# Attention followed by a gelu feed-forward on one core: weight sums loaded at another place, output tiles joined by a column order, stores at another place, nineteen added products

## The chip, the cores and the metric

The kernel runs on one core of one Trainium2 chip. The metric is the device time of one execution in microseconds (us). Before the change it was 924.78 us, the median of 3 runs (924.69 to 926.21).

The engines are called by short names. PE is TensorE (matrix products, and PEld its weight loads), DVE is VectorE, ACT is ScalarE, POOL is GpSimd, SP is SyncE. SP and ACT can issue DMA transfers, each from its own queue, in the order in which they stand there. PE writes its products to PSUM banks; the other tiles lie in SBUF.

## The reference

What is computed is an attention in which a query sees only the keys of its own cluster, and then a feed-forward layer on its output:

```python
# q, k, v: (4, 8, 768, 64); centroids: (8, 16, 64)
q_assign = argmax(einsum(q / |q|, c / |c|)); k_assign = argmax(einsum(k / |k|, c / |c|))
scores = where(q_assign[..., :, None] == k_assign[..., None, :], q @ k.T / 8, -1e9)
x = softmax(scores) @ v            # reshaped to (4 * 768, 8 * 64) = (3072, 512)
h = x @ w_in                       # w_in: (512, 2048)
g = h * sigmoid(1.702 * h)
out = g @ w_out                    # w_out: (2048, 512), out: (3072, 512)
```

All inputs and the output are float32. The weights arrive as 8-byte numbers and are brought to float32 by the kernel.

## The kernel before

The program has two stages. They are written out by hand in the order in which each engine's instructions are to stand (`manual_schedule`); a tile framework adds the waits. There is no planner. Line numbers are those of the kernel before.

**Attention**, up to about 349 us. It runs over 16 pairs of heads (`NPAIR`), each pair with its two halves of 384 queries and 6 tiles of 128 keys. One step `t` handles two key tiles: `scores` (L453) makes the score products, `part` (L467 for the first pair, L476 for the others) adds a large term that removes other clusters, `exps` (L484, ACT) takes the exponential, `add_up` (L502, POOL) sums it over the keys, `values` (L518) multiplies by v. For the first pair the preparation stands ahead of the loop: transposes of q and k (L315), products with the centroids (L341), a copy by ACT (L347), transposes back (L355), and then, after the scores of the first two tiles, `prep_hot` (L419), which transposes the one-hot tile `hot` and has `hots` copied by DVE and ACT (L424, L426). In between, the generator `rounding` (L180) turns one piece of a weight after the other to float32: pieces 0 to 15 are `w_in`, pieces 16 to 31 are rows of `w_out` with all their 512 columns. Its last step is the add at L203.

**Feed-forward**, one batch b of 768 rows after the other, 4 in all. Both products are made by a scheme with 7 products in place of 8 (two halves of each of three dimensions), which needs sums of input tiles and of weight tiles.

- `first7(b, f)` (L815), for 8 values of f: the seven products of the first layer, 14 matmuls at L822. DVE adds the PSUM results into G (L813), ACT applies the gelu (L827). Sums of the input x stand in the tiles Tx2, Tx3 and Tx4 (`T_of`) and, as T1, in x itself; they are made by `sums_x` (L608) in the order T3, T1, T2, T4. POOL makes the sums of w_in (`sums_w`).
- `second49(k)` (L858), for 7 values of k: each is again a scheme of seven products, 28 in all at L872, written as `product(bank, n, start)` with n from 1 to 7. It uses six PSUM banks in turn. The order of the outer products is `ORDER = (1, 7, 3, 2, 6, 5, 4)`. ACT copies the first result of a bank into a tile y and PE then goes on adding to that bank. For k = 0 the tile y is Y22 itself. The results go to the four output tiles Y11, Y12, Y21, Y22, by additions on POOL. Sums of G for the next k are made by `sums_t` into temporary tiles (among them E0, E1, E2 and Tx2 to Tx4), sums in G itself by `sums_G`, both on DVE at three places within `second49`, called `extra(0)`, `extra(1)` and `extra(2)`.
- **The inner weight sums.** For each k three sums of blocks of w_out are needed. In batch 0, beside `first7` with f from 3 to 7, `keep_w(k)` (L747) makes them on POOL, in the tiles Y12, Y21 and Y22, and SP stores each to memory (`kept_w`, L757). `load_sums(k)` (L761) loads them back into the tile `Wz`, of which there are two. Before the change the first two loads stand behind the last `keep_w`, after the loop over f.
- **The output.** `store(b, n, m, q)` (L918) transposes one half m of an output tile on DVE (L929), 32 by 32 elements at a time, and issues four DMAs on SP (L933), one for each group of 32 partitions. In the order of w_out's columns, each piece that is contiguous in memory is 32 numbers long. Y11 is stored beside k = 5. In batches 0 to 2 the other three tiles are stored beside the next batch's `first7` (`pend`). In the last batch Y12 and Y22 are stored at k = 6, and Y21 in parts, the last after the last product.

The sums of x for the next batch (`x_steps`) are made on DVE at k = 5 and k = 6.

## Time and profile before

| What | Value |
|---|---|
| Median of 3 runs | 924.78 us (924.69 to 926.21) |
| The profiled execution's own time | 924.83 us |
| Its span, first to last instruction | 923.0 us |
| Mean granted clock of PE | 0.984 |
| PE busy | 885.7 us, 96% of the span |
| DVE busy | 714.5 us, 77% |
| POOL busy | 485.0 us, 53% |
| ACT busy | 363.4 us, 39% |
| DMA | 204031 packets, 80.57 MB |
| Packets under 512 bytes | 180136 |

The profile is taken in one execution; its span is shorter than that execution's time by 1.83 us, which lie before the first and after the last instruction. A slice is one fortieth of the span. A digit gives the busy share of an engine in that slice, in tenths; in the row PEclk it gives the clock that was granted to PE. In a row of waits the figures are the sum, the number and the longest. In a row of the timeline the figures are the start, the length, the engine (SPq and ACTq are the queues from which SP and ACT issue), the line, the operation, the tile written and the tile read, and at the end how long the engine was idle before it and what ended that.

### The profile page before, as it was taken

Reading aid. Unit: us, or ns where it says so; the run is one execution under the profiler, and the core shown is the slowest. Engines: PE = TensorE matmul, PEld = TensorE weight load, DVE = VectorE, ACT = ScalarE, POOL = GpSimd, SP = SyncE. Lnnn points to the kernel's source line nnn. Section 1 sums busy time; section 2 is a strip of 40 time slices with the busy share of each in tenths; the row PEclk is TensorE's granted clock in tenths of the full one; section 3 lists DMA queues with packets and bytes.
Section 4 is the critical chain, followed back from the end, with each engine's and each line's share of the span. In section 5 each row is a group of like instructions: output and inputs, shape, how many; then the busy total and the mean of one; then the engine's idle time right before and its main releaser. Section 6 shows DMA issues by size and latency. Waiting matters only on the chain.

```text
span 923.0 us, 17802 instructions
## 1 busy us (share of the span) xinstructions
PE 885.7 (96%) x6693; PEld 578.3 (63%) x6693; DVE 714.5 (77%) x1165; ACT 363.4 (39%) x816; POOL 485.0 (53%) x469
## 2 busy tenths in 40 slices
PE   6999999999999999996999999999999999999991
PEld 2344444444444445555997557997557996558991
DVE  3999999998999997997797557797556796557791
ACT  3677767776667673231112222111322112222110
POOL 5799989989999898695132211132221133210140
PEclk8999999999999999998999999999999999999996
DMA  9375556666653210036323112223113123111224
GB/s 183 96 134 109 101 117 137 147 126 137 137 130 100 83 42 18 23 115 236 106 69 94 18 22 84 93 69 95 18 26 103 69 72 92 25 18 35 80 69 62
DMA packets 204031, 80.57 MB, mean 87 GB/s; under 512 B 180136, under 2 KB 186400, under 8 KB 203936
## 3 DMA queue, kind: packets, MB, share of 16 engines
q1 hardware_dynamic: 203792, 79.31, 36.5%
q8 instruction: 55, 0.90, 0.4%
q14 instruction: 40, 0.33, 0.1%
q10 hardware_dynamic: 144, 0.03, 0.0%
HBM read 62.61 MB, written 16.70 MB: 86 GB/s over the span
## 4 chain that ended last, share of the span: by engine, by line
PE 77%; DVE 6%; POOL 4%; DMA 3%; issue 3%; SPq 2%; ACT 2%; ACTq 0%; DVEq 0%; POOLq 0%
PE b L822 27%; PE b L872 24%; PE s L453 11%; PE o L518 8%; POOL Y L579 3%; PE m L535 2%; PE s L476 2%; ACT A L484 1%; DMA raw<-in_moe_w_out_dram 1%; DVE G L579 1%; SPq L404 1%; PE m L329 1%; DMA raw<-in_moe_w_in_dram 1%; POOL W L579 1%; DMA line<-row 1%
## 5 line engine op out<-in xcount | busy, mean ns | idle before, releaser
L502 POOL TENSOR_TENSOR sum<-sum,A 128x384 f32<-128x384 f32 x252 | 263.9, 1082 | 38.0 <-ACT A L484 23.8
L813 DVE TENSOR_TENSOR G<-b,G 128x384 f32<-128x384 f32 x224 | 123.0, 556 | 98.1 <-PE b L822 88.5
L484 ACT ACTIVATE A<-s 128x768 f32<-128x768 f32 x192 | 144.7, 804 | 96.6 <-PE s L476 77.8
L579 POOL TENSOR_TENSOR Y<-y,Y 128x768 f32<-128x768 f32 x28 | 63.2, 2267 | 207.5 <-DVE y L813 183.5
L453 PE MATMUL s<-T,T 64*64 64x384 f32 x1536 | 145.8, 495 | 2.7 <-ACT A L484 0.7
L827 ACT ACTIVATE G<-G 128x384 f32<-128x384 f32 x128 | 66.3, 523 | 198.4 <-DVE G L813 197.0
L518 PE MATMUL o<-A,inv 64*64 64x384 f32 x1536 | 142.1, 486 | 0.0
L579 POOL TENSOR_TENSOR W<-w_in 128x256 f32<-128x256 f32 x32 | 23.6, 736 | 161.7 <-PE b L822 161.4
L453 PEld LDWEIGHTS s<-T,T 64*64 64x64 f32 x1536 | 52.4, 132 | 80.0 <-ACT A L484 52.5
L579 DVE TENSOR_TENSOR G<-G 128x768 f32<-128x768 f32 (+1 forms) x88 | 95.8, 1111 | 0.0
L822 PE MATMUL b<-x,W 128*128 128x384 f32 x256 | 93.0, 486 | 0.0
L822 PE MATMUL b<-Tx,w_in 128*128 128x384 f32 x256 | 93.0, 486 | 0.0
L822 PE MATMUL b<-x,w_in 128*128 128x384 f32 x256 | 88.5, 486 | 0.0
L518 PEld LDWEIGHTS o<-A,inv 64*64 64x64 f32 x1536 | 58.6, 134 | 39.2 <-issue 34.4
L822 PEld LDWEIGHTS b<-x,W 128*128 128x128 f32 x256 | 48.6, 190 | 33.9
L822 PEld LDWEIGHTS b<-Tx,w_in 128*128 128x128 f32 x256 | 48.6, 190 | 33.9
L822 PEld LDWEIGHTS b<-x,w_in 128*128 128x128 f32 x256 | 48.5, 190 | 33.5 <-issue 0.6
L872 PE MATMUL b<-E,Wz 128*128 128x192 f32 x256 | 47.5, 336 | 7.3 <-DMA Wz<-kept_w 7.3
L872 PE MATMUL b<-G,w_out 128*128 128x192 f32 x288 | 50.3, 326 | 0.0
L872 PEld LDWEIGHTS b<-E,Wz 128*128 128x128 f32 x256 | 43.8, 197 | 8.5 <-ACT Y L882 7.6
L872 PEld LDWEIGHTS b<-G,w_out 128*128 128x128 f32 x288 | 47.4, 190 | 1.5 <-ACT G L827 0.3
L822 PE MATMUL b<-Tx,W 128*128 128x384 f32 x128 | 46.5, 486 | 0.0
(163 smaller groups left out, 1365.1 us busy)
## 6 DMA issues: line engine op xcount, KB each, us to landing
Wz<-kept_w SPq DMA_DIRECT2D x84, 256.0 KB
raw<-in_moe_w_in_dram SPq DMA_DIRECT2D x16, 512.0 KB
raw<-in_moe_w_out_dram SPq DMA_DIRECT2D x16, 512.0 KB
inv<-in_v_dram SPq DMA_DIRECT2D x16, 384.0 KB
in<-in_q_dram SPq DMA_DIRECT2D x60, 96.0 KB
in<-in_k_dram SPq DMA_DIRECT2D x60, 96.0 KB
kept_w<-Y SPq DMA_DIRECT2D x21, 256.0 KB
kept<-x SPq DMA_DIRECT2D x24, 192.0 KB
```

The source lines that it names most:

```text
L329: nc.tensor.matmul(out=ps[r:r + SQ, w * NJ * SQ:(w + 1) * NJ * SQ] .rearrange("p (j t) -> p j t", t=SQ), lhsT=cT[:, p % HP].rearrange("p a ...
L453: nc.tensor.matmul(out=ps[c:c + D, a, 0:HALF], lhsT=T[p, 1][rows, kt * P + c:kt * P + c + D], rhs=T[p, 0][rows, h * HALF:(h + 1) * HALF], ...
L476: nc.tensor.matmul(out=s_of[u][c:c + D, a, :], lhsT=rows_of[1, p % 2][rows, kt * P + c:kt * P + c + D], rhs=rows_of[0, p % 2][rows, h * HA ...
L484: nc.scalar.activation(out=A_of[u], in_=s_of.pop(u), func=AF.Exp, scale=SCALE)
L502: nc.gpsimd.tensor_tensor(out=sum_of[g][:, a], in0=(A_of[u - 1] if kt == 1 else sum_of[g])[:, a], in1=A_of[u][:, a], op=ALU.add)
L518: nc.tensor.matmul(out=o_of[g][a * D:(a + 1) * D, r, 0:HALF], lhsT=v_in[p][rows, a, kt, :], rhs=A[rows, a, :], start=(kt == 0), stop=(kt = ...
L535: nc.tensor.matmul(out=ps[a * D:(a + 1) * D, 0:HALF], lhsT=twos, rhs=sm[:, a, :], start=(i == 0), stop=(i == len(parts) - 1))
L579: engine.tensor_tensor(out=o, in0=a, in1=b, op=(ALU.add if op == "+" else ALU.subtract))
L813: nc.vector.tensor_tensor(out=o, in0=p, in1=a, op=ALU.add)
L822: nc.tensor.matmul(out=ps[:, 0:HALF], lhsT=a[:, c], rhs=x(c), start=(c == 0), stop=(c == 1))
L827: nc.scalar.activation(out=g, in_=g, func=AF.Gelu_apprx_sigmoid, scale=2.0)
L872: nc.tensor.matmul(out=ps, lhsT=A[n][:, f], rhs=M[n][:, f], start=start and f == 0, stop=(f == FQ - 1), skip_group_check=True)
```

## The change

It has six parts.

1. `rounding` writes the pieces of w_out with their columns in another order: column r * 128 + n * 32 + t goes to place n * 128 + r * 32 + t. The tiles of the output so hold the columns of a half m beside those of the other half: for each group r of 32 partitions, the two halves together are 64 contiguous columns.
2. `store` transposes both halves of a tile into one tile with the halves side by side, and issues four DMAs for both, with pieces of 64 numbers, where there were eight. It can share its DMAs out to two queues. The transposed tile is Tx3 for Y11, and E0, E1 and E2 for Y12, Y22 and Y21 of batches 0 to 2; in the last batch Tx3, Tx4 and Tx2.
3. Y11 is stored at the end of k = 4. The sums of x are spread over k = 5 and k = 6 in groups of 2, 2 and 4.
4. In the last batch, Y12 and Y22 are stored at the first two places of k = 6, Y21 in three parts on the queues of SP and ACT, and the additions into the output tiles of k = 4 and k = 5 are made on DVE, not on POOL.
5. `load_sums(0)` and `load_sums(1)` are issued within the loop over f, at f = 5 and f = 6.
6. `keep_busy(n)` makes n products of a bf16 identity with itself, 512 columns each, whose result nobody reads: 6 ahead of the first transpose, 3 after the centroid products, 6 ahead of `prep_hot` and 4 after it.

```diff
--- before.py
+++ after.py
@@ -200,6 +200,10 @@
         nc.vector.scalar_tensor_tensor(out=e, in0=lo, scalar=2.0 ** -52, in1=e,
                                        op0=ALU.mult, op1=ALU.mult)
         yield
+        if i >= NW // 2:
+            w, a, e = (w.rearrange("p (n r t) -> p r n t", r=P // SQ, t=SQ),
+                       *(x.rearrange("p (r n t) -> p r n t", r=P // SQ, t=SQ)
+                         for x in (a, e)))
         nc.vector.tensor_tensor(out=w, in0=a, in1=e, op=ALU.add)
 
         check_w(i, raw, w_chunks[NW - 1][0] if i < NW - 1 else raw.bitcast(
@@ -280,6 +284,16 @@
                                 op0=ALU.mult)
     cT = const.tile([P, HP, 2, NC], FP32, name="cT")
     nc.vector.memset(cT, 0.0)
+    idle = ps_o.tile([P, 2, 512], FP32, name="o")
+
+    def keep_busy(n):
+        for _ in range(n):
+            nc.tensor.matmul(
+                out=idle[:, 0, :], lhsT=ident_h,
+                rhs=ident_h[:, None, :].broadcast_to((P, 4, P)),
+                start=True, stop=True)
+
+    keep_busy(6)
     cps = bank()
     nc.tensor.transpose(out=cps[:, 0:P], in_=cc.rearrange("p a d -> p (a d)"),
                         identity=ident)
@@ -645,12 +659,16 @@
         prep(p, i)
         if p == 0 and i in (1, 3):
             load_w(i // 2)
+        if (p, i) == (0, 4):
+            keep_busy(3)
     for t in range(NT + 2):
         us = range(2 * t, 2 * t + 2) if t < NT else ()
         for u in us:
             scores(u)
         if t == 0:
+            keep_busy(6)
             prep(0, 6)
+            keep_busy(4)
         for u in us:
             part(u)
         for u in us:
@@ -855,7 +873,7 @@
             for _ in sums_t(0, slice(f - FQ, f - FQ + 1)):
                 pass
 
-    def second49(k, extra):
+    def second49(k, extra, last):
 
         i = ORDER[k]
         a, g, t, w = W_of(i), G_of(i), temps(k), W.pop(k)
@@ -906,33 +924,33 @@
             return
         nc.scalar.copy(y21, x)
         extra(2)
-        pool = nc.gpsimd
+        pool = nc.vector if last and i in (6, 5) else nc.gpsimd
         sums(pool, {1: (), 7: ((Y[21], y, "+", Y[22]),),
                     3: ((Y[12], y, "+", Y[22]),),
                     2: ((Y[11], y, "+", Y[22]),),
                     6: ((Y[12], y, "+", Y[12]), (Y[21], y, "+", Y[21])),
                     5: ((Y[12], y, "+", Y[12]), (Y[22], y, "+", Y[21]))}[i])
 
-    spare = [0]
-
-    def store(b, n, m, q=slice(0, 2)):
+    def store(b, n, m=slice(0, 2), q=slice(0, 2), queues=(nc.sync,)):
 
         h, t = divmod(n, 10)
         h, t = h - 1, t - 1
-        cols = slice(q.start * QT, q.stop * QT)
-        if b < B - 1:
-            o = ep.tile([P, HALF], FP32, name="o", bufs=1)
-        else:
-            o = T_of[2 + spare[0] // 2][:, spare[0] % 2]
-            spare[0] = (spare[0] + 1) % 6
-        o = o[:, cols]
-        nc.vector.transpose(out=o, in_=Y[n][:, m, cols])
-        rows = out[b * S + t * HALF + cols.start:b * S + t * HALF + cols.stop]
-        for r in range(0, P, SQ):
-            at = (2 * h + m) * P + r
-            nc.sync.dma_start(
-                out=rows[:, at:at + SQ].rearrange("(j t) i -> t j i", t=SQ),
-                in_=o[r:r + SQ].rearrange("t (j i) -> t j i", i=SQ))
+        o = {11: T_of[3], 12: E[0], 22: E[1], 21: E[2]} if b < B - 1 else {
+            11: T_of[3], 12: T_of[3], 22: T_of[4], 21: T_of[2]}
+        o = o[n].rearrange("p a t -> p (a t)").rearrange(
+            "p (j m i) -> p j m i", m=2, i=SQ)
+        at, to = q.start * QT, q.stop * QT
+        o = o[:, at // SQ:to // SQ]
+        for one in range(m.start, m.stop):
+            nc.vector.transpose(out=o[:, :, one], in_=Y[n][:, one, at:to])
+        rows = out[b * S + t * HALF + at:b * S + t * HALF + to]
+        for r in range(P // SQ):
+            col = r * P + (2 * h + m.start) * SQ
+            queues[r % len(queues)].dma_start(
+                out=rows[:, col:col + (m.stop - m.start) * SQ].rearrange(
+                    "(j t) i -> t j i", t=SQ),
+                in_=o[r * SQ:(r + 1) * SQ, :, m].rearrange(
+                    "t j m i -> t j (m i)"))
 
     okt = const.tile([1, 1], FP32, name="okt")
     bad = const.tile([1, 1], I32, name="bad")
@@ -976,10 +994,9 @@
                 for k in {3: (0,), 4: (1, 2), 5: (3,), 6: (4, 5),
                           7: (6,)}[f]:
                     keep_w(k)
+                if 5 <= f < 7:
+                    load_sums(f - 5)
         after7(FB - 1)
-        if b == 0:
-            load_sums(0)
-            load_sums(1)
         if b < B - 1:
             for h in range(2):
                 for hp in range(HP):
@@ -990,28 +1007,25 @@
         else:
             made = iter(())
 
-        def stores(b, *todo):
+        def stores(b, *todo, **how):
             for n in todo:
-                for m in range(2):
-                    store(b, n, m)
-                    yield
+                store(b, n, **how)
+                yield
+
+        both = dict(queues=(nc.sync, nc.scalar))
 
         def tail():
-            store(b, 21, 0)
-            store(b, 21, 1, slice(1, 2))
+            for n in (12, 22):
+                store(b, n)
+                yield
+            store(b, 21, slice(0, 1), slice(0, 1), **both)
+            store(b, 21, q=slice(1, 2), **both)
             yield
 
         def chain(*todo):
             for steps in todo:
                 yield from steps
 
-        def mixed(one, two):
-            for _ in one:
-                yield
-                for _ in range(3):
-                    next(two, None)
-                    yield
-
         def sums_of_x():
             for XT[:] in made:
                 yield
@@ -1021,10 +1035,9 @@
 
         for k in range(7):
             nxt = sums_t(k + 1) if k < 6 else iter(())
-            more = {1: sums_G(6), 3: sums_G(5), 4: sums_G(4),
-                    5: mixed(stores(b, 11), x_steps),
-                    6: chain(x_steps, stores(b, 12, 22), tail()) if final else
-                    x_steps}.get(k, iter(()))
+            more = {1: sums_G(6), 3: sums_G(5),
+                    4: chain(sums_G(4), stores(b, 11)), 5: x_steps,
+                    6: tail() if final else x_steps}.get(k, iter(()))
             if b == B - 1 and k < 2:
                 test(k)
             if (b, k) == (B - 1, 6):
@@ -1032,17 +1045,17 @@
 
             def extra(at):
                 do(nxt, (2, 1, 1)[at])
-                do(more, ((3, 1, 1) if final else (3, 3, 3))[at] if k == 6
-                   else (0, 3, 3)[at] if k == 5 else (0, 2, 2)[at])
-
-            second49(k, extra)
+                do(more, ((1, 1, 1) if final else (0, 4, 4))[at] if k == 6
+                   else (0, 2, 2 + (k == 4))[at])
+
+            second49(k, extra, final)
             if k < 5:
                 load_sums(k + 2)
             elif b < B - 1:
                 load_sums(k - 5)
         pend = () if final else stores(b, 12, 22, 21)
         if final:
-            store(b, 21, 1, slice(0, 1))
+            store(b, 21, slice(1, 2), slice(0, 1), **both)
     return is_bad
 @with_exitstack
 def general(
```

## The prediction

> **What bounds the kernel now.** I read the page's slices first, then the waits of TensorE (PE), then stretches of the timeline where those waits stand.
>
> ```profile
> PE   6999999999999999996999999999999999999991
> PEclk8999999999999999998999999999999999999996
> ...
> PE b L872 <- DMA Wz<-kept_w: 7.3, 1, 7.3
> PE m L284 <- DVE cT L282: 4.9, 1, 4.9
> PE m L419 <- DVE hot L375: 1.4, 1, 1.4
> ```
>
> PE is busy in 37 of 40 slices (each 23 us). Only the first slice, the one at 415 to 438 us and the last have holes. All of PE's listed waits sum to under 17 us; the rest of the hole is after its last matmul (about 903.5 of a 923.0 us span). So a faster DVE, ACT or DMA in the middle gives nothing: what counts is PE's start, one stall, and what follows PE's end. The change touches all three, and edits the order of DVE's work in between.
>
> **Start: the clock.** I cut the beginning where the granted clock changes (columns: PE, PEld, DVE, ACT, POOL busy, then PEclk, DMA share, GB/s):
>
> ```profile
> 8.66:12.07 3.41, 2.84 (x27) 0.96 (x21) 1.11 (x2) 0.68 (x2) 3.20 (x5) 1.00 1.48 178
> 12.07:15.48 3.41, 1.15 (x18) 0.74 (x16) 3.32 (x6) 0.80 (x1) 1.17 (x2) 1.00 1.21 235
> 15.48:18.90 3.42, 2.84 (x20) 0.88 (x20) 1.31 (x2) 1.51 (x2) 0.00 (x0) 0.50 1.18 220
> 18.90:22.31 3.41, 3.41 (x24) 0.93 (x20) 0.00 (x0) 1.51 (x2) 1.21 (x2) 0.50 1.37 176
> ```
>
> After a stretch with PE busy 1.15 of 3.41 us (it waited 1.36 us for `hot`, 0.90 us for `hots`) the clock is half for 6.8 us, and the same 16 score matmuls that took 1.52 us at 10.80 take 2.84 us at 16.83. The 19 added products (6, 3, 6 and 4) stand in these holes. They have no row. Nearest by kind are the 12 products of L419, 128 columns in bf16: 0.86 us, 0.072 us each with start-up; nearest by length are the one-pass costs behind L822, where 384 float32 columns take 0.32 us, hence at most 0.43 us for 512 and, if bf16 needs half the passes, 0.21 us. I take 0.21 us, since four times the L419 cost less its start-up is near it; 0.43 us is the upper bound. The first six (1.3 us, at most 2.6) start when `ident_h` is there at 1.57 and end before the first transpose at 4.92: covered. Three (0.64 us) stand in the 0.57 us wait for the copy at L347: 0.1 us late. Six (1.28 us) fill the 1.36 us wait, four (0.85 us) the 0.90 us wait. Cost: about 0.15 us on the path; at 0.43 us each it would be 0.7 + 1.2 + 0.8 = 2.7 us.
>
> What a full clock gives: following the queue from 15.44, the part products take 0.50 instead of 0.82 us, the exponentials follow 0.3 us sooner, scores of the next two tiles end at 18.25, their part at 18.75, the 16 value products (1.52 instead of 2.46) at 20.25, so the score group at 23.53 starts near 21.0: 2.5 us, less 0.15, **2.4 us**. It passes on: in each later 20.5 us period PE is busy over 20.3 us, while DVE and POOL hold 18.5, so nothing else takes over. The Trainium skill ("TensorE: Matmul & The Clock Gate", What's actually happening, and its closing table) says that the half clock follows an idle window of about 3.4 us and that only gaps over some 3 us matter. By that rule these products buy nothing, because the gaps are 1.36 and 0.90 us, and the sum would be 2.4 us smaller. The rows speak against its threshold: a window one third full was enough. I follow the rows.
>
> **The inner weight sums.** The 21 stores of `keep_w` and the loads after them share SP's queue. Moving `load_sums(0)` and `load_sums(1)`, three loads each, ahead of the last `keep_w` calls delays those stores by 6 issues of some 0.4 us, but they wait for POOL anyway.
>
> ```profile
> 426.83 1.38 POOL L579 TENSOR_TENSOR Y<-w_out,Y 128x512 f32<-128x512 f32 x1
> 428.60 2.81 SPq L764 DMA_DIRECT2D Wz<-kept_w  x6
> 429.19 0.36 DVE L579 TENSOR_TENSOR E<-Y,G 128x192 f32<-128x192 f32 x1
> 430.37 0.32 ACT L882 COPY Y<-b 128x192 f32<-128x192 f32 x1 [6.70 <-DMA kept_w<-Y]
> 431.65 4.64 PE L872 MATMUL b<-E,Wz 128*128 128x192 f32 x16 [7.34 <-DMA Wz<-kept_w]
> ```
>
> The load goes, but the 7.3 us do not. For the first product the output tile `y` is Y22 itself, which is also the staging tile of the last `keep_w` sum. POOL finishes that at 428.21, its store lands at 430.3, and only then may ACT copy PSUM to Y22 (its row names that DMA). PE's next product adds to the same PSUM bank, so it waits for this copy: 430.37 + 0.32 = 430.69. PE can start at about 430.75 instead of 431.65. Gain **0.9 us**. The half clock after the stall stays (16 products in 4.64 us against 2.76 elsewhere): 6.4 us of idle are still long.
>
> **Transitions to the next batch.** Output of Y11 moves from product k=5 to the end of k=4, into Tx3, and the x sums then write Tx3 first.
>
> ```profile
> 478.78 5.05 DVE L579 TENSOR_TENSOR G<-G 128x768 f32<-128x768 f32 x2
> 488.93 4.46 POOL L579 TENSOR_TENSOR Y<-y,Y 128x768 f32<-128x768 f32 x2 [5.92 <-DVE y L813]
> 489.54 2.18 DVE L579 TENSOR_TENSOR x<-x 128x384 f32<-128x384 f32 x1
> 494.00 1.01 DVE L579 TENSOR_TENSOR Tx<-x 128x384 f32<-128x384 f32 x2
> 495.92 1.45 PE L822 MATMUL b<-Tx,W 128*128 128x384 f32 x4
> ```
>
> DVE has no hole here, and Tx2 is ready at 495.01, 0.9 us before PE needs it. In the new order: two transposes (0.57 us, overlapped 0.5) end at 484.9; four issues at 0.47 + 0.05 us end at 487.0; landing takes 1.4 (a 3 KB store) to 1.9 us (below), so 488.4 to 488.9. DVE, after four sums and two small adds, arrives at 488.3 and waits 0.1 to 0.6 us. Queued behind it: two Tx3 sums, the add into y that starts POOL, the sum E2, the x sums. POOL starts near 490.0 instead of 488.93; a two-input DVE sum beside it ends only as POOL's operation does (2.18 and 1.67 us for 0.5 of work), so the x sums end near 494.9 and, after two adds, Tx2 near 496.3. PE wants its halves at 495.92 and 496.28: 0 to 0.4 us late, **0.2 us** taken, three times: +0.6. The sums that PE's last products need (E0, E1, E2) stay 0.9 us or more ahead. Bounds: 0, and 1.3 us if DVE waits 0.9 us longer.
>
> The pairs of transposes in the next batch's first groups (1.1 us at once) find 0.73 us of DVE idle in every 1.29 us and six PSUM banks; without that cover each could hold PE up to 0.5 us. The permuted write of the rounded w_out has no row; the plain one takes 0.69 us. Even at double cost, two in a period add 1.4 us to DVE's 18.5 of 20.5 us: no cost taken.
>
> **The tail.**
>
> ```profile
> 896.33 22.10 SPq L933 DMA_DIRECT2D out_dram<-Tx  x36
> 902.04 1.46 PE L872 MATMUL b<-E,w_out 128*128 128x192 f32 x8
> 904.13 0.32 DVE L813 TENSOR_TENSOR Y<-b,Y 128x192 f32<-128x192 f32 x1
> 905.77 0.38 DVE L929 STREAM_TRANSPOSE Tx<-Y 128x192 f32<-128x192 f32 x1 [1.32 <-DMA out_dram<-Tx]
> ```
>
> SP issues 36 stores at 0.61 us each, to 918.43; 4.57 us later the span ends. DVE finished at 906.2: the issue is the bound (the DMA share is 0.3 to 0.65). The new order has 4 stores for Y11 at k=4, 4 each for Y12 and Y22, and 12 for Y21 over SP and ACT. DVE in k=4 of this batch loses POOL's competition (5.06 us of G sums become 1.82) and gains four Y sums of 0.94: even. Y12 is transposed by 899.7 and issued by 901.9; y's last quarter but one comes from PE at 900.9, so Y22 is transposed by 902.7 and Y21's parts at 904.0, 904.7 and, after PE's end, 905.4. SP unhindered would end at 907.0. But in the built order SP's third and fourth Y22 stores wait for ACT's first two stores to land (one semaphore lane serves both, one DMA after the other): ACT issues at 904.05 to 904.8 (0.35 each for a half), landing 1.87 later as in the trace (a store issued by 903.77 frees its tile at 905.64), so SP goes on at 906.3: two at 0.52, six at 0.4, end 909.7. Gain 918.43 - 909.7 = **8.7 us**; bounds 11.4 (no such wait) and 7.5 (landing 2.5 us).
>
> **Sum.** -2.4 - 0.9 + 0.6 - 8.7 = -11.4 us. Profiled execution 924.83 (span 923.0 and 1.83 around it), 0.05 above the median of 924.78. **Predicted 913.4 us.**
>
> **Rivals.** (1) *DVE's new wait on the Tx3 stores becomes PE's*: for it, DVE's gapless row; against, landing in 1.4 to 1.9 us. At 1.3 us a transition: 913.4 + 3.3 = 916.7. (2) *The added products don't hold the clock* or cost what they win; the skill's threshold speaks for it, the one-third window against: 915.8. (3) *The 7.3 us stall goes wholly*, with its half clock (6.4 + 1.8 more): 905.2; the ACT row speaks against it. (4) *Slower*: the same wait of DVE on Tx3, if 48 KB in pieces of 256 bytes land 6.1 us after the last issue: each us beyond 1.9 costs three, 4.2 us a transition, 926.0; it decides from 5.7 us on. Against it: 1.87 us measured in a full queue.
>
> **Numbers.** Forecast 0.63, rival 1 0.18, rival 2 0.11, rival 3 0.04, rival 4 0.03, 0.01 for no difference. 910.0 to 917.0 holds the first three with the tail's bounds. Faster 0.96, same 0.01, slower 0.03; 0.2% (1.8 us) is about what runs of this kernel can tell (924.69 to 926.21).
>
> **What would show it.** Clock 1.00 until 424 us and the first full score period 2 to 2.5 us sooner; the stall still over 6 us, released by ACT's copy to Y22; DVE idle at the Tx3 sum for under 0.6 us, named after the store; last store issued some 6 us after PE's end. Wrong: a half clock before 30 us, PE waiting for Tx2, or SP issuing 12 us after PE's end.

## The result, and the profile after

The changed kernel took 915.19 us (median of 5 runs, 913.93 to 918.32) where the kernel before took 925.18 us in the same comparison (5 runs, 924.69 to 926.21). The ratio is 0.9893, with a 95% interval of 0.9871 to 0.9914. The forecast was 913.4 us with a range of 910 to 917. One of the five runs lies outside that range. The later experiments point to the reason: the kernel has a wait that the prediction did not see, and it comes and goes between executions.

The profiled execution took 914.16 us, with a span of 912.4 us. Lines of the changed kernel are those of the kernel before plus 14 to 18 (L872 is now L890, L882 is L900, L453 is L467, L579 is L593, L822 is L840, L933 is L949, L764 is L782).

The page's slices, after:

```profile
PE   8999999999999999997999999999999999999994
PEclk9999999999999999998999999999999999999998
```

PE's waits (sum, number, longest):

```profile
PE b L890 <- ACT Y L900: 6.4, 1, 6.4
PE o L291 <- DVE ident_h L245: 1.6, 1, 1.6
```

The clock digit of the first slice rose from 8 to 9. The one long wait is still there at 6.4 us, but it is now named after ACT's copy. The last slice is less empty.

The four stretches in which the clock had been lost (columns as before: PE, PEld, DVE, ACT, POOL busy, granted clock, DMA share, GB/s):

```profile
8.66:12.07 3.41, 3.41 (x30) 1.22 (x27) 0.90 (x2) 0.91 (x2) 3.14 (x6) 1.00 1.38 174
12.07:15.48 3.41, 3.41 (x30) 1.51 (x22) 3.31 (x7) 0.67 (x1) 1.39 (x2) 1.00 1.18 237
15.48:18.90 3.42, 2.68 (x30) 0.69 (x28) 1.54 (x2) 1.74 (x4) 0.00 (x0) 1.00 1.16 227
18.90:22.31 3.41, 3.41 (x50) 1.39 (x48) 1.05 (x2) 1.41 (x2) 2.56 (x3) 1.00 1.37 175
```

The timeline of PE over the added products and the first full score group:

```profile
1.63 2.74 PE L291 MATMUL o<-ident_h 128*128 128x512 bf16 x6 [1.63 <-DVE ident_h L245]
...
9.92 0.82 PE L291 MATMUL o<-ident_h 128*128 128x512 bf16 x3
...
12.48 1.47 PE L291 MATMUL o<-ident_h 128*128 128x512 bf16 x6
...
14.70 1.04 PE L291 MATMUL o<-ident_h 128*128 128x512 bf16 x4
...
16.91 1.58 PE L467 MATMUL s<-T,T 64*64 64x384 f32 x16 [0.74 <-ACT A L498]
...
21.09 1.52 PE L467 MATMUL s<-T,T 64*64 64x384 f32 x16
```

The six products ahead of `prep_hot` take 1.47 us, 0.245 us each, close to the 0.21 us taken in the prediction. The first six take 0.46 us each, more than its upper bound of 0.43 us, but they end at 4.37, before PE's next work at 5.14, and cost nothing. The clock is 1.00 in all four stretches, and the score group that began at 23.53 begins at 21.09, 2.44 us sooner. From the score group before it (16.83 and 16.91) the way there shrank from 6.70 to 4.18 us.

A clock of 1.00 in such a row can also mean that the trace has no record. The changed kernel's clock records begin only at 9.20 us, and PE works at half its later pace before: 0.46 us for a product that takes 0.245 us afterwards.

The add that now writes w_out in another order takes 0.69 us (L207), as it did before, so that part cost nothing.

The timeline of the stall at the start of the second products, and of one transition to the next batch:

```profile
428.01 0.32 ACT L900 COPY Y<-b 128x192 f32<-128x192 f32 x1 [6.66 <-DMA kept_w<-Y]
428.39 4.85 PE L890 MATMUL b<-E,Wz 128*128 128x192 f32 x16 [6.38 <-ACT Y L900]
...
475.11 6.59 POOL L593 TENSOR_TENSOR Y<-y,Y 128x768 f32<-128x768 f32 x2 [7.12 <-DVE y L831]
475.72 1.82 DVE L593 TENSOR_TENSOR G<-G 128x768 f32<-128x768 f32 x2
478.52 1.92 SPq L949 DMA_DIRECT2D out_dram<-Tx  x4
480.55 11.19 SPq L782 DMA_DIRECT2D Wz<-kept_w  x9
485.07 2.76 PE L890 MATMUL b<-E,Wz 128*128 128x192 f32 x16
```

PE restarts at 428.39 instead of 431.65; 2.44 us of that come from the start, 0.82 us from the earlier load. The wait is now for the copy to Y22, and the copy for the store of the last kept sum. In the transition DVE's two sums in G take 1.82 us and POOL's additions 6.59 us. Before the change it was 5.05 us on DVE; POOL's addition beside these sums took 4.85 us. This turns out to matter.

The end, first the timeline, then the wait of SP's queue for earlier stores after 895 us:

```profile
896.29 11.27 SPq L949 DMA_DIRECT2D out_dram<-Tx  x14
900.97 3.61 ACTq L949 DMA_DIRECT2D out_dram<-Tx  x6
```

```profile
SPq L949 <- DMA out_dram<-Tx: 2.0, 2, 1.8
```

PE ends at 900.45 (before: 903.50), SP's last store is issued at 907.56 (before: 918.43) and the span ends at 912.36 (before: 923.03). From PE's end to the span's end it was 19.53 us and is 11.91 us. So of the profile's 10.67 us, 2.44 come from the clock, 0.82 from the load and 7.62 from the end, and 0.21 are lost again by the half clock after the stall (16 products in 4.85 us instead of 4.64).

### The profile page after: what moved, and what is told of

Same layout as the page of the kernel before. It is cut to its first block, busy times and chain, and to the rows that moved or that the text cites. A ratio compares the mean times of both kernels' runs of the same rounds, so it can differ in the third digit from the quotient of the medians.

```text
span 912.4 us, 17739 instructions
## 1 busy us (share of the span) xinstructions
PE 888.9 (97%) x6712; PEld 580.8 (64%) x6712; DVE 712.0 (78%) x1170; ACT 363.2 (40%) x816; POOL 481.1 (53%) x465
## 4 chain that ended last, share of the span: by engine, by line
PE 82%; DVE 5%; POOL 4%; DMA 3%; issue 2%; SPq 2%; ACT 2%; ACTq 0%; DVEq 0%; POOLq 0%
PE b L840 28%; PE b L890 28%; PE s L467 11%; PE o L532 9%; POOL Y L593 3%; PE m L549 2%; PE s L490 2%; ACT A L498 1%; DMA raw<-in_moe_w_out_dram 1%; SPq L418 1%; PE m L343 1%; DMA raw<-in_moe_w_in_dram 1%; POOL W L593 1%; DMA line<-row 1%; DVE x L570 1%
## 5 line engine op out<-in xcount | busy, mean ns | idle before, releaser
L593 POOL TENSOR_TENSOR Y<-y,Y 128x768 f32<-128x768 f32 x24 | 59.4, 2483 | 186.8 <-DVE y L831 162.9
L467 PE MATMUL s<-T,T 64*64 64x384 f32 x1536 | 144.6, 491 | 2.6 <-ACT A L498 0.9
L593 POOL TENSOR_TENSOR W<-w_in 128x256 f32<-128x256 f32 x32 | 23.5, 735 | 164.5 <-PE b L840 164.2
L467 PEld LDWEIGHTS s<-T,T 64*64 64x64 f32 x1536 | 52.3, 132 | 78.6 <-ACT A L498 51.5
L840 PE MATMUL b<-x,W 128*128 128x384 f32 x256 | 93.0, 486 | 0.0
L840 PE MATMUL b<-Tx,w_in 128*128 128x384 f32 x256 | 93.0, 486 | 0.0
L840 PE MATMUL b<-x,w_in 128*128 128x384 f32 x256 | 88.5, 486 | 0.0
L593 DVE TENSOR_TENSOR G<-G 128x768 f32<-128x768 f32 (+1 forms) x88 | 84.3, 980 | 0.0
L840 PEld LDWEIGHTS b<-x,W 128*128 128x128 f32 x256 | 48.6, 190 | 33.9
L840 PEld LDWEIGHTS b<-Tx,w_in 128*128 128x128 f32 x256 | 48.6, 190 | 33.9
L840 PEld LDWEIGHTS b<-x,w_in 128*128 128x128 f32 x256 | 48.5, 190 | 33.5 <-issue 0.6
L890 PE MATMUL b<-E,Wz 128*128 128x192 f32 x256 | 47.7, 337 | 6.4 <-ACT Y L900 6.4
L890 PE MATMUL b<-G,w_out 128*128 128x192 f32 x288 | 50.3, 326 | 0.1
L890 PEld LDWEIGHTS b<-E,Wz 128*128 128x128 f32 x256 | 44.0, 197 | 7.5 <-ACT Y L900 6.7
L890 PEld LDWEIGHTS b<-G,w_out 128*128 128x128 f32 x288 | 47.4, 190 | 1.5 <-ACT G L845 0.4
L840 PE MATMUL b<-Tx,W 128*128 128x384 f32 x128 | 46.5, 486 | 0.0
```

Source lines behind the costliest of these rows:

```text
L467: nc.tensor.matmul(out=ps[c:c + D, a, 0:HALF], lhsT=T[p, 1][rows, kt * P + c:kt * P + c + D], rhs=T[p, 0][rows, h * HALF:(h + 1) * HALF], ...
L593: engine.tensor_tensor(out=o, in0=a, in1=b, op=(ALU.add if op == "+" else ALU.subtract))
L840: nc.tensor.matmul(out=ps[:, 0:HALF], lhsT=a[:, c], rhs=x(c), start=(c == 0), stop=(c == 1))
L890: nc.tensor.matmul(out=ps, lhsT=A[n][:, f], rhs=M[n][:, f], start=start and f == 0, stop=(f == FQ - 1), skip_group_check=True)
```

## The experiments

Each run has a median over four to seven executions, and one profiled execution. The last two columns are from the profiles: stalls of 1.36 to 1.59 us of PE at k = 6, explained below, and the time from PE's end to the span's end.

| Run | Median us (range) | Ratio to before (95%) | Late transitions | PE end to span end |
|---|---|---|---|---|
| the change | 915.19 (913.93 to 918.32) | 0.9893 (0.9871 to 0.9914) | 0 of 3 | 11.91 |
| e1 | 921.49 (919.41 to 922.87) | 0.9951 (0.9939 to 0.9964) | 2 | 11.98 |
| e2 | 918.93 (915.34 to 921.99) | 0.9927 (0.9905 to 0.9949) | 1 | 11.94 |
| e3 | 919.29 (916.93 to 922.77) | 0.9927 (0.9909 to 0.9945) | 3 | 13.13 |
| e4 | 917.29 (912.80 to 920.28) | 0.9907 (0.9885 to 0.9929) | 2 | 12.39 |
| e5 | 916.15 (915.64 to 917.51) | 0.9905 (0.9892 to 0.9918) | 0 | 13.78 |
| e6 | 914.22 (913.84 to 915.01) | 0.9886 (0.9871 to 0.9900) | 0 | 12.62 |
| e7, the change again | 919.45 (917.33 to 921.56) | 0.9942 (0.9926 to 0.9958) | 3 | 12.30 |
| e8 | 922.20 (922.14 to 923.52) | 0.9973 (0.9962 to 0.9984) | 0 | 18.89 |
| e9 | 912.67 (912.22 to 913.76) | 0.9867 (0.9848 to 0.9886) | 0 | 10.41 |
| e10 | 917.84 (917.12 to 918.16) | 0.9919 (0.9905 to 0.9934) | 0 | 13.95 |
| e11 | 916.66 (916.08 to 918.06) | 0.9909 (0.9894 to 0.9924) | 0 | 13.90 |

The start of an execution moves by up to 1.8 us: in the kernels with added products the second group of scores (L467) begins between 15.95 and 17.76 us. Most of this goes with the clock. The first record of a full clock lies at 4.84 us in e7, 9.20 in the change and 11.08 in e9, and the group begins at 15.95, 16.91 and 17.76. From there to PE's restart after the long stall the kernels with the same loads and all added products agree closely: between 411.37 us (e5) and 411.56 us (e3), with 411.48 in the change. So stages are compared below from that group where it matters.

### e1: no added products

```diff
     def keep_busy(n):
-        for _ in range(n):
+        for _ in range(0):
```

> The changed kernel without its nineteen added products; all else stays. Theory (a window with PE busy one third brings the half clock): the half clock is back for some 6.8 us from about 15 us on, PE reaches the 16 score matmuls of the third step at about 23.5 us instead of 21.1, and span and median are 2.0 to 2.6 us longer than the changed kernel's 912.4 and 915.19. Rival (only idle gaps of some 3 us matter, the gain at the start comes from something else): clock 1.00 throughout the start, within 0.3 us of the changed kernel.

The clock is lost again, in the last of the stretches where it was lost before the change:

```profile
15.48:18.90 3.42, 1.78 (x20) 0.74 (x22) 1.86 (x4) 2.31 (x3) 0.00 (x0) 0.95 1.29 211
18.90:22.31 3.41, 3.41 (x28) 1.03 (x28) 0.80 (x1) 1.38 (x2) 0.43 (x1) 0.55 1.35 183
```

The timeline of PE has the score groups at the start, and PE's restart:

```profile
12.14 2.84 PE L467 MATMUL s<-T,T 64*64 64x384 f32 x16
...
18.06 2.40 PE L467 MATMUL s<-T,T 64*64 64x384 f32 x16 [0.74 <-ACT A L498]
...
430.89 3.56 PE L890 MATMUL b<-E,Wz 128*128 128x192 f32 x10 [6.39 <-ACT Y L900]
```

PE restarts at 430.89 instead of 428.39, 2.50 us later, but this is not one loss of the size forecast. The half clock on record lasts 3.4 us (18.56 to 21.97), half as long as before the change, and from the second score group to the restart it costs 1.35 us (412.83 against 411.48). The other 1.15 us lie ahead of that group. This execution's clock records begin only at 15.14, later than in any other profile, and its first score group takes 2.84 us, the half-clock time, where the change's takes 1.52. Whether the added products would have brought the full clock sooner there is not shown: with all of them the first record lies anywhere between 4.30 and 11.08 us. The median is 6.3 us above the change's, but two waits of 1.53 and 1.36 us at later products stand in its profile which the change's profile does not have. They became the question of the next runs.

### e2: the two first loads back behind the last kept sum

```diff
-                if 5 <= f < 7:
-                    load_sums(f - 5)
         after7(FB - 1)
+        if b == 0:
+            load_sums(0)
+            load_sums(1)
```

> The changed kernel with the first two loads of inner weight sums back behind the loop over f. Theory (the copy into Y22 bounds the stall, the load ends only 0.9 us later): PE's stall grows from 6.4 to about 7.3 us and its release is named after the DMA into Wz again; span 0.7 to 1.2 us longer. Rival (the early load took away the whole stall and something new filled it): more than 3 us longer.

The wait goes back to the load (timeline of ACT and PE):

```profile
427.25 0.32 ACT L900 COPY Y<-b 128x192 f32<-128x192 f32 x1 [6.67 <-DMA kept_w<-Y]
...
428.41 4.28 PE L890 MATMUL b<-E,Wz 128*128 128x192 f32 x16 [7.18 <-DMA Wz<-kept_w]
```

ACT's copy ended at 427.57, and PE went on 0.84 us later, when the load had landed. From the second score group (here at 16.26) it is 412.15 us, against 411.4 to 411.5 with the early loads: 0.7 us. The prediction had 0.9. One late transition stands in this profile too (1.57 us), so the median of 918.93 cannot be set against 915.19 for this part alone.

### e3: the last tile's stores on one queue

```diff
-        both = dict(queues=(nc.sync, nc.scalar))
+        both = dict(queues=(nc.sync,))
```

> The changed kernel with all twelve stores of Y21 on SP, none on ACT. Theory (ACT's stores make SP's third and fourth Y22 stores wait for them, through a shared semaphore lane, so the second queue gives nothing): SP's 20 last stores go on without the 1.8 us wait, the last one is issued between 906.5 and 907.9 (907.6 in the changed kernel), span within 0.8 us of 912.4. Rival (the second queue carries half of the tail): six more stores at 0.4 to 0.6 us on SP, 2.4 to 3.6 us longer.

The end grew from 11.91 to 13.13 us. Profiles with the same tail code as the change show 11.91 to 12.39 us (change, e1, e2, e4, e7), so the second queue is worth 0.7 to 1.2 us, less than the rival's 2.4 to 3.6. SP then waits for no lane (a lane is one of eight semaphores that the stores of both queues take in turn, so that a store first waits for the one that had the lane last), but issues 20 stores in a row. This profile has three late transitions, which are more than the rest of the median's 4.1 us.

### e4: the last kept sum staged in a tile of its own

```diff
+            if (k, i) == (6, 2):
+                o = ep.tile([P, 2, HALF], FP32, name="y").rearrange(
+                    "p a t -> p (a t)")[:, 0:FQ * P].rearrange(
+                    "p (f n) -> p f n", n=P)
             sums(nc.gpsimd, ((o, x, op, z),))
```

> The changed kernel with the last inner weight sum staged in a y tile that is still free, instead of in Y22. Theory (the copy into Y22 is what PE waits for): ACT copies some 0.3 us after PE's second product, and PE goes on when DVE has the first E0, at about 427.3 us instead of 428.4; stall about 5.3 us, span 0.8 to 1.4 us shorter. Rival (the copy is only named, POOL or the DMA of the weights bounds): stall and span as in the changed kernel within 0.3 us. If nothing else bounded PE there, the stall would go and the span be 6 us or more shorter.

The timeline of ACT and PE at the stall:

```profile
422.04 0.32 ACT L904 COPY Y<-b 128x192 f32<-128x192 f32 x1 [0.20 <-DMA kept_w<-Y]
...
422.41 0.92 PE L894 MATMUL b<-E,Wz 128*128 128x192 f32 x4
423.98 0.59 PE L894 MATMUL b<-E,Wz 128*128 128x192 f32 x2 [0.65 <-DVE E L593]
427.78 3.44 PE L894 MATMUL b<-E,Wz 128*128 128x192 f32 x10 [3.21 <-DVE E L593]
...
431.06 1.46 PE L894 MATMUL b<-Y,w_out 128*128 128x192 f32 x8
```

With the copy freed from the store, PE starts at 422.41 and stops at what is late next, DVE's sums E beside POOL. The next product stands at 431.06 instead of 433.07, and 2.6 us sooner when both are measured from the second score group. That confirms what ends the stall in the changed kernel: the copy into the tile whose store has not landed, and not the load. Of the wait 0.65 and 3.21 us are left, for DVE's sums.

This profile also has a half clock close to its start, with all added products in place. The rows are of the stretches between its clock records:

```profile
4.30:7.72 3.42, 1.81 (x14) 1.35 (x13) 1.20 (x7) 0.99 (x3) 3.21 (x5) 1.00 1.35 175
7.72:11.13 3.41, 3.29 (x14) 0.89 (x13) 0.00 (x0) 1.37 (x3) 3.22 (x5) 0.50 1.35 174
```

The first six products had ended at 4.37 and the next three began at 10.09, so none stood in that hole. Its second score group begins at 17.54, 1.3 us later than in e2 (16.26), whose full clock came at about the same time and stayed.

### What the scatter is made of

The runs of e4 lie 7.5 us apart, those of the kernel before beside them 1.75 us (11 runs, 925.07 to 926.82). The start's 1.8 us are too little for that. The profiles differ at one more place. Beside k = 4, DVE's two sums in G and POOL's additions into Y run at the same time, and in the executions seen one or the other is held back: either POOL's take 4.85 us and DVE's 5.05 us, or DVE's 1.82 us and POOL's 6.59 us. In the change's profile DVE was the quick one at all three transitions and there is no stall; in e1 to e4 there is one stall of 1.36 to 1.59 us for each transition at which DVE was slow, and none for the others. All stand at the same products of k = 6 (b<-E,Wz), named after the load of Wz in five of the eight and after a DVE instruction in three. Behind slow sums Y11 is transposed late, its four stores are issued late, and behind them on SP's queue stand the loads of the weight sums for k = 6. Before the change these loads stood ahead of Y11's stores. The next four runs, on one chip, test this.

### e5: the loads for k = 6 ahead of Y11's stores

```diff
+        def loads_then(k, steps):
+            load_sums(k)
+            yield from steps
...
-                    4: chain(sums_G(4), stores(b, 11)), 5: x_steps,
+                    4: chain(sums_G(4), loads_then(6, stores(b, 11))),
+                    5: x_steps,
...
-            if k < 5:
+            if k < 4:
                 load_sums(k + 2)
-            elif b < B - 1:
+            elif k > 4 and b < B - 1:
```

> The changed kernel, but at k = 4 the loads of the weight sums for k = 6 are issued ahead of Y11's four stores, as they stood before the change. Theory (new, from the profiles of the changed kernel and of the first four experiments): in those executions in which DVE's two sums of G beside k = 4 go behind POOL's addition (5.05 instead of 1.82 us), Y11's stores go out some 1.3 us late and the loads behind them on SP's queue with them, and PE stalls 1.4 to 1.6 us at the sixth product of k = 6, up to three times in an execution. With the loads first no such stall is left whichever way the sums of G go: the median is 913.5 to 914.5, and the runs lie within 2 us of each other, as those of the kernel before do. Rival A: what makes PE late is DVE's wait for the Tx3 stores, not the loads; then the stalls stay, 1.3 to 1.6 us each, and the runs scatter over 914 to 919 as before. Rival B: the loads ahead make Y11's stores land later still, DVE waits 1 us longer for Tx3 at each transition and PE waits for Tx2: 915 to 917 with little scatter.

### e7: the changed kernel again, beside it

> The changed kernel itself once more, as a control on the same chip. Theory: each execution has zero to three of the 1.5 us stalls, so the runs scatter from 914 to 918.5, about 1.5 us apart, median 914 to 917; a profile shows as many stalls as it has pairs of G sums at k = 4 that take 5.05 us. Rival: the scatter seen so far came from the chip, and all runs lie within 2 us of 914.

The timeline of one transition of e7, where the loads come last:

```profile
474.18 4.86 POOL L593 TENSOR_TENSOR Y<-y,Y 128x768 f32<-128x768 f32 x2 [7.12 <-DVE y L831]
474.79 5.06 DVE L593 TENSOR_TENSOR G<-G 128x768 f32<-128x768 f32 x2
...
480.82 1.92 SPq L949 DMA_DIRECT2D out_dram<-Tx  x4
482.85 9.76 SPq L782 DMA_DIRECT2D Wz<-kept_w  x9
484.64 1.03 DVE L593 TENSOR_TENSOR Tx<-x 128x384 f32<-128x384 f32 x2 [0.61 <-DMA out_dram<-Tx]
485.88 2.84 PE L890 MATMUL b<-E,Wz 128*128 128x192 f32 x16 [1.57 <-DMA Wz<-kept_w]
```

The same transition of e5, which began 1.5 us later in its execution:

```profile
473.23 2.15 SPq L782 DMA_DIRECT2D Wz<-kept_w  x3
476.06 4.85 POOL L593 TENSOR_TENSOR Y<-y,Y 128x768 f32<-128x768 f32 x2 [7.12 <-DVE y L831]
476.68 5.05 DVE L593 TENSOR_TENSOR G<-G 128x768 f32<-128x768 f32 x2
482.71 1.93 SPq L949 DMA_DIRECT2D out_dram<-Tx  x4
486.03 2.76 PE L890 MATMUL b<-E,Wz 128*128 128x192 f32 x16
486.41 1.03 DVE L593 TENSOR_TENSOR Tx<-x 128x384 f32<-128x384 f32 x2 [0.49 <-DMA out_dram<-Tx]
```

DVE's sums are as slow in e5 as in e7, and DVE waits nearly as long for Tx3 (0.49 us against 0.61), but the loads were issued at 473.23 and PE does not wait. So the load's place on SP's queue is the cause of the stalls, and DVE's wait for Tx3 is not. e5 is free of them at all three transitions, and its runs lie within 1.9 us. Its median lies where rival B put it, but not for that rival's reason: PE's product with Tx2 is only 0.05 us late at the transition shown. Three stalls (1.57, 1.55 and 1.41 us) make 4.5 us; the medians of e5 and e7 differ by only 3.3 us because e5 lost 1.5 us at the end, 13.78 us against 12.30. SP's waits after 895 us in e5:

```profile
SPq L949 <- DMA out_dram<-Tx: 6.3, 3, 3.2
```

It was 2.1 us in e7. The tail's own code is the same, and only three loads were moved, but the traces show the stores on other lanes. In e5 the first two stores of Y22 stand behind lanes that ACT's stores hold (5.0 us), and the fourth of Y12 waits 1.3 us for SP's own second. Without the 1.5 us e5's median would be close to the 913.5 to 914.5 us that were expected. e7, in turn, came out above the median of 914 to 917 us that was expected of it. Its profile has as many stalls as slow sums, as forecast; whether all its executions had three of them isn't known.

### e6: both, and Y22 on two queues

To e5's edit and e4's comes this one:

```diff
-                store(b, n)
+                store(b, n, **(both if n == 22 else {}))
```

> The kernel of the run with the loads ahead of Y11's stores, and two edits more: the last kept weight sum is staged in a tile of its own, so that ACT's copy to Y22 doesn't wait for a store; and Y22's four last stores are shared between SP and ACT, so that none of SP's waits behind a lane that ACT holds. Theory: 2.0 to 2.5 us less at the stall (PE goes on at 431.0 instead of 433.1 when its start is the same, as the run with that edit alone showed), and 1 to 2.5 us less at the end (SP's wait of 2.0 us goes), so 909 to 911, and a spread under 2 us. Rival: the tail is bound by the landing of the last stores, not by SP's wait, and gains nothing: 911.5 to 912.5.

The median is 1.9 us under e5's, less than either case said. At the stall the next product stands 2.6 us sooner from the second score group, but its eight matmuls take 2.08 us where e5's take 1.46, since the half clock now reaches into them; 2.0 us remain. At the end SP still waits 6.0 us for lanes (1 to 2.5 us of gain were expected from that wait's going, and it did not go), and the end is 1.2 us shorter than e5's.

### e8: the two halves stored apart in the last batch

e5's kernel, with each store of the last batch issued as two of 32 numbers a piece:

```diff
-            queues[r % len(queues)].dma_start(
+            for one in (range(m.start, m.stop) if b == B - 1 else (None,)):
+                mm = m if one is None else slice(one, one + 1)
+                to_col = col + (0 if one is None else (one - m.start) * SQ)
+                queues[r % len(queues)].dma_start(
```

> The kernel with the loads ahead of Y11's stores, but in the last batch each store is issued for one half of a tile alone, in pieces of 32 numbers as before the change: twice as many DMAs with the same bytes, in the same order. It tells how much of the tail's gain comes from the joined halves and how much from the earlier place. Theory (the issue of stores is the tail's bound): 12 to 14 more issues on SP's queue behind Y12's transposes, of 0.4 to 0.5 us each, less the 2.0 us in which SP waits for a lane now: 3 to 6 us more than the run with the loads ahead of the stores. Rival (the place bounds it, since PE's last products free the tiles): within 1 us of that run.

6.05 us more than e5, at the theory's upper edge. From PE's end to the span's end it is 18.89 us: of the 19.53 us before the change, the earlier places and the second queue alone take away 0.6, and joining the halves takes the next 5.1. Of these 5.1 us 4.1 lie ahead of the last issue (13.11 us after PE's end, for 9.04) and 1.0 behind it. So the issuing of the stores is most of what bounds the end. The run makes the pieces smaller as well as the stores more, and does not tell the two apart.

### e9: Y12 on two queues as well

```diff
-                store(b, n, **(both if n == 22 else {}))
+                store(b, n, **both)
```

> The kernel of three edits (loads ahead of Y11's stores, the last kept sum staged elsewhere, Y22 on two queues), with Y12's four last stores shared between SP and ACT as well, so that the two queues take turns and each of the eight lanes goes back to the queue that held it. Theory: the tail is bound by SP's waits for lanes that ACT's stores hold (2.0 us in the changed kernel, 6.3 us in the run with the loads ahead, 6.0 us with Y22 shared). With them gone each queue has ten stores of 0.46 us, the last is issued some 3.5 us after PE's end in place of 7.9, and the span ends 8 to 9 us after PE's end in place of 12.6: 909.5 to 911. Rival: the landing of the stores bounds it; lanes then wait for their own queue's stores and the end stays at 11 us or more: 913 to 914.5.

The timeline of ACT and PE ahead of the end:

```profile
894.90 0.90 ACTq L953 DMA_DIRECT2D out_dram<-Tx  x2
895.84 0.32 ACT L910 COPY y<-b 128x192 f32<-128x192 f32 x1 [4.18 <-PE b L894]
896.21 1.57 PE L894 MATMUL b<-G,w_out 128*128 128x192 f32 x8 [1.05 <-ACT y L910]
```

And SP's wait for earlier stores:

```profile
SPq L953 <- DMA out_dram<-Tx: 1.8, 2, 1.2
```

SP's wait for lanes falls from 6.0 to 1.8 us and the end from 12.62 to 10.41 us, not to the 8 to 9 expected: the last store is issued 6.1 us after PE's end, not 3.5, since SP still waits 1.8 us, now for stores of its own queue to land, and single issues take 0.8 to 1.3 us. And there is a new wait: ACT issues two stores of Y12 at 894.90, its copy of a PSUM bank stands behind them on its queue, and PE waits 1.05 us for the copy. 912.67 us is the lowest median of the study. Its interval lies clear of e7's (0.9942), but overlaps those of e6 and of the change's first comparison.

### e10 and e11: parts of e5

e10 leaves out the first six and the three added products; e11 has POOL make the last batch's additions again.

```diff
-    keep_busy(6)
     cps = bank()
...
-            keep_busy(3)
+            pass
```

> The kernel with the loads ahead of Y11's stores, with only the six and four added products around prep_hot; the first six and the three are left out. Theory: it is the window around prep_hot (PE 1.15 of 3.41 us busy) that cost the clock, so these ten hold it: clock 1.00 until the feed-forward, the same median as the run with the loads ahead within 1 us (915 to 917). Rival: the first nine are needed too, since the window that counts starts earlier; then a half clock shows before 25 us and the time is 2 to 2.5 us above that run: 918 to 919.5.

From the first clock record, at 10.87 us, the clock is 1.00 up to 32 us, and from the second score group to the restart it is 411.40 us as in the others. The ten products around `prep_hot` were enough to hold the clock there. Whether the other nine bring the full clock sooner can't be told from one profile, with a first record that moves as it does. The median is 1.2 us above e11's on the same chip and 1.7 above e5's; the profiles show no place for it (their spans are 916.2 and 915.7 us), and it stays open.

```diff
-        pool = nc.vector if last and i in (6, 5) else nc.gpsimd
+        pool = nc.gpsimd
```

> The kernel with the loads ahead of Y11's stores, with the last batch's additions into the output tiles of k = 4 and k = 5 back on POOL. The prediction called the move to DVE even. Theory: within 0.7 us of the run with the loads ahead (915.5 to 917), since PE waits for neither engine there; DVE's sums of G take 5.05 us again in the last batch. Rival: with POOL's additions Y12 and Y22 are finished later than the tail needs them and the end moves out by 1 to 3 us (917 to 919), or Y11's stores come late and stall the last batch.

0.5 us above e5 in the medians, on another chip, and 0.1 us less in the spans: even, as the prediction said.

## Why the prediction was right, and where it was not

**The clock.** Right in mechanism, and in size for the profile that it was read from: 2.44 us in the change's profile, 2.4 forecast. That e1 gives 2.50 us is chance, since it is made of 1.35 us for a half clock of half the length and 1.15 us for a later start. The sum took the before profile's 6.8 us of half clock as fixed, and both the length and the start move between executions. The prediction followed the rows against a rule: the Trainium skill ("TensorE: Matmul & The Clock Gate", What's actually happening) ties the half clock to an idle window of about 3.4 us, by which these gaps were harmless. e1's rows have 1.78 of 3.42 us busy and a clock of 0.55 in the next stretch, with no wait of PE there longer than 0.9 us. e4 has 1.81 of 3.42 us busy and 0.50 next, and e2, with 2.00 us busy (4.68 to 8.09), kept its clock. The measurement decides against the threshold: stretches with 1.15, 1.78 and 1.81 us busy were followed by the half clock, and PE's longest wait in them was 1.36 us. e4 also has the half clock before 30 us that the prediction named as a sign of being wrong, in a hole that no added product fills. Ten of the nineteen products were enough in e10.

**The inner weight sums.** Right: the load's wait went and the copy's took its place, named as forecast. 0.8 us in the change and 0.7 us in e2, for 0.9. e4 shows that the copy ended the 6.4 us that were left, and that DVE's sums stand only 2.6 us behind it, so rival 3 (the whole stall goes) had no ground.

**The transitions.** The priced wait is there, but the step was incomplete. DVE waits 0.5 to 0.8 us for Tx3 where POOL goes first, where 0.1 to 0.6 was forecast, and it costs PE 0.05 us at one transition of e5 (two weight loads for Tx2 wait 0.42 and 0.17 us) and 0.2 us at one of e8 and of e11, for the 0.2 us taken for each. What was missed is in the sentence that puts four issues of Y11's stores at the end of k = 4: it followed DVE, which waits for them, and not SP's queue, on which `load_sums(6)` stood behind them from now on. Where DVE's sums of G come second that costs PE 1.4 to 1.6 us a transition, up to 4.5 us. The prediction also took DVE's slow case (5.05 us) as given, and the profiled execution had the quick one, so its own transitions show no loss at all, where the sum had 0.6 us.

**The tail.** Right in mechanism, too large by 1.1 us: 7.6 us instead of 8.7. SP did wait for ACT's stores to land, for 2.0 us: 1.8 us ahead of the third store of Y22, so that the fourth came right behind it, and 0.2 us at one of Y21. Then the last eight stores took 4.92 us to issue (0.61 each) where the sum had 3.4: single ones took 0.32 to 0.46 us, but some 0.88 and 1.10. And the span ended 4.80 us after the last issue instead of 4.57.

**The total.** 914.16 us profiled and 915.19 us in the median stand against 913.4, with the tail's 1.1 us as the main difference; the 0.6 us that the transitions did not cost work against it. But the agreement of the median is in part luck, in which executions were met: e7, the same kernel, has a median of 919.45 us, outside the range, in a profile with all three stalls. Its mechanism stood in none of the cases.

**Rivals.** Rival 1 gave 1.3 us more a transition, which is close to what e7 shows, but for another reason (DVE's wait for Tx3). Rival 2 doesn't stand: without added products the clock was lost around `prep_hot` in both profiles (before and e1), with the ten around it in none of eleven. Rival 4 needed a landing of more than 5.7 us; DVE waited at most 0.8 us for it, in any run.

## What to carry to other kernels

When a step that issues DMAs is moved, list what stands behind those DMAs on the issuing queue, not only who waits for the moved data: here a load that nobody had touched came late and cost PE 1.5 us. Give a queue's urgent loads their place before stores whose time depends on a contest between two engines. And when stores of one tile leave from two queues, look at which earlier store each has to wait for: a change elsewhere can shift the lanes and cost the tail 1.5 us. And before two executions are compared, find out when each one's full clock began: here that alone moved the start by more than 1 us.

## What had not been expected of the hardware

In the transition of e7 and that of the change, both shown above, POOL's first addition starts 0.26 us after one of DVE's sums and 0.61 us before the next, and still it goes two ways. In e7 POOL gets through first (2.37 and 2.53 us, DVE's sums in G then 2.57 us each); in the change's profile DVE's two sums take 0.95 us each and POOL's addition stays 4.11 us. The Trainium skill ("SBUF — State Buffer", Who interferes with whom) says that a DVE instruction with two inputs in SBUF contends with POOL's reads for a pair of ports that is an exclusive lock, and that the order of issue decides who blocks. The durations fit the lock; the order of issue does not tell these two cases apart, whose starts agree to 0.01 us. All 21 transitions of e5 to e11 and the three of e3 had DVE slow, the three of the change's first profile had DVE quick, and e1, e2 and e4 had both within one execution. What decides it wasn't found.

The price of a store's issue was the other surprise: most take 0.32 to 0.49 us, but close to the end single ones take 0.8 to 2.0 us with no wait named.
